# Retention and a softplus feed-forward on one core: five plain and three seven-product pairs of weight blocks in the first pass

## The chip, the cores and the metric

The kernel runs on one core of a Trainium2 chip. The metric is the device time of the whole program in microseconds (us), the median of three timed runs. Engines are called PE (TensorE's matmuls; PEld is its weight load), DVE (VectorE), ACT (ScalarE), POOL (GpSimd) and SP (SyncE, whose queue issues all the DMAs spoken of here). Each engine takes its instructions in the order in which the program has them.

## The reference

Causal retention (attention without softmax, with a decay per head) on 8 batches, 8 heads, 576 tokens, 64 columns per head, and on its result, seen as 4608 tokens by 512 features, a two-layer network with a softplus between:

```python
ret = (q @ k.transpose(0, 1, 3, 2) / np.sqrt(64)) * Dmat      # Dmat = gamma_h ** (i - j) for i >= j, else 0
x = (ret @ v).transpose(0, 2, 1, 3).reshape(4608, 512)
h = x @ w_in                                                  # w_in: 512 x 2048
g = np.maximum(h, 0.0) + np.log1p(np.exp(-np.abs(h)))         # softplus
out = g @ w_out                                               # w_out: 2048 x 512
```

All of it is in float32. For the matmuls every operand is split in a head that the PE takes whole and the rest (HI and LO), and a product is three: LO by HI, HI by LO, HI by HI.

## The kernel before

**Tiling.** The 4608 tokens are nine units of 512. Unit 0 runs while the weights are still being split. The units after it go two at a time: a super-step takes the units 2s+1 and 2s+2 and all 2048 hidden columns. The change touches the first super-step (units 1 and 2); units 3 to 8 run in `full_pair` and `full_phase` and are left as they are. The hidden columns are 16 blocks of 128, in eight pairs J.

**Plain slots and seven-product pairs.** For a plain pair, h is computed once per unit and block: `plain_slot(u, p, xa, xb, ...)` does two products (lines 847 to 851, six matmuls of 512 columns each) for block p of unit u, then the softplus on ACT and DVE, the split of g, and the output products (`output_some`, line 500, twelve matmuls) of the block before. That makes eight products for a pair and both units. `strassen_pair` computes the same four results (two blocks, two units) by Strassen and Winograd's scheme with seven products, from sums of x and sums of the weights. Its products are, in order, B11 and T2, T3, NT4 into the PSUM bank `acc`, B21 into `two`, T1 and B22 into `third`; ACT and DVE put them together in the four parts c[0] to c[3] and take the softplus of each. The results for unit 2 are written out to DRAM (`kept`) and fetched again in the second pass (`kept_parts`), which then has only their output products to do.

**The two passes.** The first pass is unit 1: plain slots p = 0 to 11 (the pairs 0 to 5, PLAIN = 6) and then the seven-product pairs 6 and 7. The second is unit 2: twelve plain slots and the kept parts of the two pairs. The retention for coming tokens is done in groups (`chunk_products`, lines 209 to 299), one in every second slot and one in each pair: its small matmuls write the scores into `two` and the sums into `third`; DVE empties them (`scores_out` L243, `halves_out` L429, `states_out` L271 to L281). A pair's group asks at its end for the next group's keys and values (`queue_steps`): keys at once, the other three loads one by one with the next products.

**Sums.** The seven-product scheme wants sums of x, made from `xs` by `combined_x` (L447 to L450, one column of 128 tokens at a time, on POOL) and split by `combined_parts` (ACT L454, DVE L455). It wants sums of the weights too: `w_in`'s for a pair in this super-step before the pair runs, all of `w_in`'s and `w_out`'s for units 3 to 8. A set of them is two additions of 128 by 512 (L633 or L648), four of 128 by 256 (L658 to L661), a head on ACT (L665, two), a rest on DVE (L669, two) and two stores of 512 KB (L677).

**What sets the order.** Engine queues follow the program text. Which of these steps stands in which slot is written out by hand in tables: `schedule((slot, step, ...), ...)` for the two passes, `extras` for the seven-product pairs. Weight blocks come through a ring of seven tiles (`block_load`, L619): each product, when it is issued, asks for the block seven products ahead. Tiles called quad are nine; DMAs take turns on eight semaphores, and one waits for the one before it on its own.

Of the kernel before, what the change touches and what calls it, by code (L numbers as in the profile page):

```python
# [54 lines left out]
PLAIN = 6  # L55
# [28 lines left out]
def retention_softplus_ffn(ctx: ExitStack, tc, first, whole, others, consts, w, out):  # L84
# [831 lines left out]
    def prepare_rest(j):  # L916
        combine_rest(raws[j])
# [25 lines left out]

    def start_combined(i, engine=nc.gpsimd):
        tmps[i] = quad().rearrange("p n (a b c) -> p (n a) b c", a=2, b=2)
        combined_x(tmps[i], column(i), engine)
# [10 lines left out]
    def half_b22(i):  # L957
# [5 lines left out]
        (1, prepare, PLAIN + 1), (1, prepare_whole, PLAIN), (2, prepare_sums, PLAIN), (3, prepare_split, PLAIN),  # L963
        (3, half_b22, 0), (4, prepare_store, PLAIN), (4, prepare_whole, PLAIN + 1), (4, prepare_sums, PLAIN + 1),
        (5, finish_combined, 0, nc.vector), (5, half_b22, 1), (6, prepare_split, PLAIN + 1),
        (6, prepare_ring, 4, 0, 3, 2), (7, prepare_store, PLAIN + 1), (7, prepare_ring, 4, 3, 4, 3),
        (7, finish_combined, 1, nc.vector), (7, half_b22, 2), (8, prepare_sums, 4), (9, prepare_ring, 5),
        (9, finish_combined, 2, nc.vector), (10, prepare_split, 4), (10, prepare_sums, 5), (10, half_b22, 3),
        (11, prepare_store, 4), (11, finish_combined, 3, nc.vector), (11, prepare_head, 5),
        (0, whole_out, 0), (1, combine_out, 0), (2, split_out, 0), (3, store_out, 0),  # L970
        *[(5 + 2 * j, raw_store, j) for j in range(4)])
    starts = schedule(*[(3 + 2 * i, start_combined, i) for i in range(CPU)])
    for p in range(2 * PLAIN):
        group = groups.pop() if p % 2 == 0 and p < 10 else None
        plain_slot(1, p, B11, B21, rest, group, (), *(x.get(p, ()) for x in (jobs, starts)))
# [6 lines left out]
    def strassen_pair(s, J, group, rest, last=False, extra=None):  # L982
# [12 lines left out]
        if extra is not None:  # L995
            whole_out(extra)
        for j in stores:
            prepare_rest(j)
        if last:
            half_x(B12, STAGE[0, 1], slice(0, T), nc.gpsimd)  # L1000
        ab = None if J == PLAIN else logs(c[0])
        output_some(-(-len(outputs) // 4))
        while stores:
            prepare_store(stores.pop(0))
        product(z, T1, True)
        nc.scalar.copy(c[1], z)  # L1006
        ab = ab or logs(c[0])
        softplus(c[0], ab)
        if extra is not None:
            combine_out(extra)  # L1010
        product(acc, T2)
        nc.scalar.copy(c[2], acc)
        if extra is not None:
            combine_head(raws["out", extra])
# [10 lines left out]
        if extra is not None:  # L1025
            combine_rest(raws["out", extra])
# [4 lines left out]
        nc.scalar.copy(c[3], acc)  # L1031
        ab4 = logs(c[3])
# [7 lines left out]
        if group:  # L1040
            chunk_products(*group, None)
            coming_steps = next_steps(group[0]) if s == 0 and J == NJ - 1 else []
            if extra is not None:
                combine_store(outs_dram[extra], raws.pop(("out", extra)))
            group_out(*group, between=(finish,))
            for k in coming_steps:
                scale_values(k)
# [14 lines left out]
    stores = [5]  # L1062
# [7 lines left out]
    extras = {(0, NJ - 2): 1, (0, NJ - 1): 2}  # L1070
    for s in range(FULL):
# [3 lines left out]
        for J in range(first, NJ):  # L1075
            rest, kept = strassen_pair(s, J, groups.pop() if groups else None, rest, s == 0 and J == NJ - 1,
                                       extras.get((s, J)))
# [10 lines left out]
        if first:  # L1088
            blocks = schedule((0, prepare_ring, 0))
            plan = schedule(  # L1090
                *[(2 * j - 1, prepare_ring, j) for j in range(1, 4)], *[(2 * j, prepare_sums, j) for j in range(4)],
                *[(2 * j + 1, prepare_split, j) for j in range(4)], *[(2 * j + 2, prepare_store, j) for j in range(4)],
                *[(8 + 2 * i, finish_combined, i, nc.vector) for i in range(2)],
                (9, half_x, B21, STAGE[1, 0], whole, nc.vector), *[(2 * j - 7, raw_store, j) for j in range(4, NJ)],
                (4, whole_in, 3, 0), (6, combine_out, 3), (7, split_out, 3), (8, store_out, 3),
# [318 lines left out]
```

## Time and profile before

| | |
|---|---|
| three timed runs | 834.57 us median (832.39 to 835.04) |
| the profiled execution's own time | 834.83 us, of which 833.0 us from the first to the last instruction |
| PE busy | 816.8 us (98%), 7322 instructions |
| DVE, ACT, POOL busy | 644.3 (77%), 546.8 (66%), 164.3 us (20%) |
| granted TensorE clock, mean | 0.998 |
| DMA | 209.93 MB, 252 GB/s |

Busy PE time counts overlapping matmuls whole, so short waits hide in it: how fast matmuls follow one another is read from the starts of a timeline's rows. A row with "x12" is twelve instructions merged, with the start of the first. What stands in brackets is idle time before it and what ended it. In the order rows below, a name is the tile, `xt` the split x, `xs` the x before the split, `quad` the tiles of sums and of c, `wout` the split `w_out`, `ab` and `g` the softplus before and after its split.

### The profile page before, as it was taken

What the parts mean: (1) busy time and instruction counts of PE and PEld (TensorE: products, weight loads), DVE (VectorE), ACT (ScalarE), POOL (GpSimd) and SP (SyncE); (2) the same over time, 40 slices, a digit from 0 to 9 for tenths busy, and PEclk for the clock granted to TensorE, in tenths of its full rate; (3) what the DMA queues carried; (4) which work ended last, traced back from release to release, by engine and by line L of the source; (5) the groups of instructions that cost most, each with busy time, mean ns of one, the idle gap of its engine ahead of it and who ended that gap; (6) DMA issues with size and microseconds to landing.
All of it is one profiled execution on the core that took longest, in us unless ns stands there. A gap on an engine that the chain in (4) does not pass through costs nothing.

```text
span 833.0 us, 19064 instructions
## 1 busy us (share of the span) xinstructions
PE 816.8 (98%) x7322; PEld 667.2 (80%) x7322; DVE 644.3 (77%) x1068; ACT 546.8 (66%) x957; POOL 164.3 (20%) x228
## 2 busy tenths in 40 slices
PE   8999999999999999999999999999999999999998
PEld 6788888887778888888887887888778888888886
DVE  5899976878787885878989985777789955555886
ACT  6788765456754544777777556767675658878653
POOL 3322221540221452111113000112110002212100
PEclk9999999999999999999999999999999999999999
DMA  9888879887799984697887777778657686666675
GB/s 357 311 284 304 314 247 359 293 300 247 244 317 343 334 281 150 221 307 253 284 267 260 215 228 235 252 235 261 195 159 213 205 254 190 195 194 193 194 214 172
DMA packets 149258, 209.93 MB, mean 252 GB/s; under 512 B 10800, under 2 KB 114736, under 8 KB 149168
## 3 DMA queue, kind: packets, MB, share of 16 engines
q1 hardware_dynamic: 149168, 208.72, 76.1%
q8 instruction: 58, 0.95, 0.4%
q14 instruction: 32, 0.26, 0.1%
HBM read 166.74 MB, written 41.94 MB: 251 GB/s over the span
## 4 chain that ended last, share of the span: by engine, by line
PE 73%; DVE 14%; ACT 8%; DMA 2%; issue 2%; SPq 0%; DVEq 0%; ACTq 0%
PE sum L1153 17%; PE acc L849 16%; PE y L500 12%; PE third L849 9%; PE two L849 4%; PE two L1153 3%; PE acc L1153 2%; PE third L1153 2%; PE h L466 2%; ACT ab L477 2%; PE third L225 2%; ACT parts L1143 2%; DVE g L1163 1%; DVE parts L1147 1%; ACT ab L473 1%
## 5 line engine op out<-in xcount | busy, mean ns | idle before, releaser
L849 PE MATMUL acc<-xt,ring 128*128 128x512 f32 x768 | 194.4, 391 | 1.0 <-DVE quad L1022 0.6
L1153 PE MATMUL sum<-parts,ring 128*128 128x512 f32 x720 | 174.9, 394 | 1.6 <-ACT ab L478 1.6
L849 PEld LDWEIGHTS acc<-xt,ring 128*128 128x128 f32 x768 | 143.9, 188 | 33.5 <-ACT g L1176 1.4
L1143 ACT CAST parts<-g 128x512 fp32r<-128x512 f32 x168 | 102.9, 621 | 88.5 <-DVE g L1163 28.4
L1153 PEld LDWEIGHTS sum<-parts,ring 128*128 128x128 f32 x720 | 134.6, 189 | 30.3 <-DVE xs L429 1.5
L1147 DVE TENSOR_TENSOR parts<-g,parts 128x512 fp32r<-128x512 f32 x168 | 117.7, 722 | 38.1 <-ACT parts L1143 36.2
L500 PE MATMUL y<-wout,g 128*128 128x512 f32 x576 | 140.1, 392 | 0.3 <-DVE g L493 0.3
L500 PEld LDWEIGHTS y<-wout,g 128*128 128x128 f32 x576 | 107.1, 188 | 23.3 <-PE h L466 0.7
L849 PE MATMUL third<-xt,ring 128*128 128x512 f32 x444 | 111.2, 390 | 0.0
L849 PEld LDWEIGHTS third<-xt,ring 128*128 128x128 f32 x444 | 83.2, 188 | 17.9 <-ACT quad L1006 0.4
L478 ACT ACTIVATE ab<-ab 128x512 f32<-128x512 f32 x120 | 75.9, 632 | 3.8
L477 ACT ACTIVATE ab<-ab 128x512 f32<-128x512 f32 x120 | 75.9, 633 | 3.5
L1163 DVE SCALAR_TENSOR_TENSOR g<-g,ab 128x512 f32<-128x512 f32 x96 | 67.4, 713 | 7.7 <-ACT ab L478 7.5
L202 POOL TENSOR_TENSOR qv<-qv,consts_sb 128x256 f32<-128x256 f32 x61 | 44.2, 726 | 116.9 <-DMA qv<-others 109.2
L489 ACT CAST g<-ab 128x512 fp32r<-128x512 f32 x44 | 27.3, 621 | 45.3 <-DVE ab L485 24.4
L466 PE MATMUL h<-xt,win 128*128 128x512 f32 x192 | 47.3, 395 | 1.3 <-DVE x L410 0.7
L493 DVE TENSOR_TENSOR g<-ab,g 128x512 fp32r<-128x512 f32 x44 | 32.7, 742 | 18.0 <-ACT g L489 17.2
L283 POOL TENSOR_TENSOR s<-s,consts_sb 128x256 f32<-128x256 f32 (+1 forms) x31 | 20.4, 657 | 127.2 <-DVE s L281 109.8
L473 ACT ACTIVATE ab<-g 128x512 f32<-128x512 f32 x72 | 45.0, 625 | 0.0
L849 PE MATMUL two<-xt,ring 128*128 128x512 f32 x168 | 42.8, 391 | 0.8 <-DVE xs L429 0.8
L1252 POOL TENSOR_TENSOR g<-g 128x512 f32<-128x512 f32 x10 | 14.1, 1409 | 149.1 <-DVE g L1163 149.1
L466 PEld LDWEIGHTS h<-xt,win 128*128 128x128 f32 x192 | 35.3, 188 | 9.4 <-DVE win L587 1.5
(191 smaller groups left out, 1340.5 us busy)
## 6 DMA issues: line engine op xcount, KB each, us to landing
ring<-split SPq DMA_DIRECT2D x126, 256.0 KB, 4.6
ring<-combined SPq DMA_DIRECT2D x104, 256.0 KB, 3.5
ring<-outcombined SPq DMA_DIRECT2D x96, 256.0 KB, 3.4
qv<-others SPq DMA_DIRECT2D x61, 320.0 KB, 4.9
ring<-outsplit SPq DMA_DIRECT2D x72, 256.0 KB, 3.6
wst<-w SPq DMA_DIRECT2D x32, 512.0 KB, 5.6
keys<-others SPq DMA_DIRECT2D x61, 256.0 KB, 5.1
split<-win SPq DMA_DIRECT2D x16, 512.0 KB, 6.0
```

What stands on the lines that cost most here:

```text
L202: nc.gpsimd.tensor_mul(v, v, f.unsqueeze(2).broadcast_to([P, 4, D]))
L466: nc.tensor.matmul(h, wins[p][:, a, kt * P:(kt + 1) * P], xt[:, b, T1 + kt // 2, kt % 2], start=(n == 0), stop=(n == 3 * NKT - 1))
L473: nc.scalar.activation(ab, h, AF.Abs)
L477: nc.scalar.activation(ab, ab, AF.Exp, scale=-1.0)
L478: nc.scalar.activation(ab, ab, AF.Ln, bias=1.0)
L493: nc.vector.tensor_sub(g[:, LO], ab, g[:, HI].bitcast(F32))
L500: nc.tensor.matmul(ys[u][tt], g[:, a, tt * P:(tt + 1) * P], wouts[p][:, b], start=(p == 0 and n == 0), stop=(p == NF - 1 and n == 2))
L849: nc.tensor.matmul(bank, w[:, ta, kt * P:(kt + 1) * P], xt[:, tb, x, kt], start=start and k == 0, stop=k == 5, skip_group_check=True)
L1143: nc.scalar.copy(t[:, HI], g_slot(J, n))
L1147: nc.vector.tensor_sub(t[:, LO], g_slot(J, n), t[:, HI].bitcast(F32))
L1153: nc.tensor.matmul(bank[m], w[:, a, m * P:(m + 1) * P], t[:, b], start=start and n == 0, stop=n == 2, skip_group_check=True)
L1163: nc.vector.scalar_tensor_tensor(c, c, 0.0, ab, op0=ALU.max, op1=ALU.add)
```

## The change

Five pairs are plain in the first super-step and three are seven-product pairs (5, 6 and 7). The sums of x are made on DVE, two columns of 128 tokens in one instruction (`start_wide`, `finish_wide`). The sums of `w_in` for pair 7 and those of `w_out` for pairs 1 to 4 are made inside the three seven-product pairs (`work`), up to two sets in each. Pair 4's `w_in` sums move to the second pass, and B12's rest in the last pair goes from POOL to DVE.

```diff
-PLAIN = 6
+PLAIN = 5
...
+    def start_wide(i, half):
+
+        b11, b12, b21, b22 = (later["xs"][:, STAGE[n], :, wide(i)] for n in ((0, 0), (0, 1), (1, 0), (1, 1)))
+        t = quad().rearrange("p n (b c) -> p n b c", b=2)
+        if half == 0:
+            nc.vector.tensor_sub(t[:, 0], b12, b11)
+            nc.vector.tensor_sub(t[:, 1], b22, b12)
+        else:
+            nc.vector.tensor_sub(t[:, 0], b22, tmps[i, 0][:, 0])
+            nc.vector.tensor_sub(t[:, 1], b21, t[:, 0])
+        tmps[i, half] = t
+
+    def finish_wide(i, half):
+        at = slice(T1 + 2 * half, T1 + 2 * half + 2)
+        hi, lo = (xt[:, n, at, :, wide(i)] for n in (HI, LO))
+        t = tmps[i, half]
+        nc.scalar.copy(hi, t)
+        nc.vector.tensor_sub(lo, t, hi.bitcast(F32))
+
+    def in_sums(j):
+        return [lambda f=f: f(j) for f in (prepare_whole, prepare_sums, prepare_head, prepare_rest, prepare_store)]
+
+    def out_sums(j):
+        return [lambda: whole_out(j), lambda: combine_out(j), lambda: combine_head(raws["out", j]),
+                lambda: combine_rest(raws["out", j]), lambda: store_out(j)]
...
-    starts = schedule(*[(3 + 2 * i, start_combined, i) for i in range(CPU)])
+        (9, finish_wide, 1, 0), (9, start_wide, 1, 1), (9, finish_wide, 1, 1), (9, half_b22, 3),
+        *[(3 + 2 * j, raw_store, j) for j in range(4)])
+    starts = {}
...
@@ strassen_pair @@
-        if extra is not None:
-            whole_out(extra)
-        for j in stores:
-            prepare_rest(j)
+        for f in work[0][:2] if work else ():
+            f()
         if last:
-            half_x(B12, STAGE[0, 1], slice(0, T), nc.gpsimd)
-        ab = None if J == PLAIN else logs(c[0])
+            half_x(B12, STAGE[0, 1], slice(0, T), nc.vector)
         output_some(-(-len(outputs) // 4))
-        while stores:
-            prepare_store(stores.pop(0))
         product(z, T1, True)
         nc.scalar.copy(c[1], z)
-        ab = ab or logs(c[0])
+        ab = logs(c[0])
         softplus(c[0], ab)
-        if extra is not None:
-            combine_out(extra)
         product(acc, T2)
         nc.scalar.copy(c[2], acc)
-        if extra is not None:
-            combine_head(raws["out", extra])
+        for f in work[0][2:3] if work else ():
+            f()
...
         softplus(c[2], ab2)
-        if extra is not None:
-            combine_rest(raws["out", extra])
+        for f in work[1][:2] if len(work) > 1 else ():
+            f()
...
         nc.scalar.copy(c[3], acc)
+        for f in work[1][2:3] if len(work) > 1 else ():
+            f()
         ab4 = logs(c[3])
...
-            if extra is not None:
-                combine_store(outs_dram[extra], raws.pop(("out", extra)))
             group_out(*group, between=(finish,))
+            for n in range(3, 5):
+                for fs in work:
+                    fs[n]()
...
-    extras = {(0, NJ - 2): 1, (0, NJ - 1): 2}
+    work = {(0, PLAIN): (in_sums(PLAIN + 2), out_sums(1)), (0, PLAIN + 1): (out_sums(2), out_sums(3)),
+            (0, PLAIN + 2): (out_sums(4),)}
...
@@ second pass @@
-                (4, whole_in, 3, 0), (6, combine_out, 3), (7, split_out, 3), (8, store_out, 3),
-                (8, whole_in, 4, 1), (9, combine_out, 4), (10, split_out, 4), (11, store_out, 4))
+                (9, prepare_head, 4), (9, stores.append, 4), (3, half_x, B21, STAGE[1, 0], whole, nc.vector),
```

Three places show how the instructions move. First ACT, from the last plain slot's softplus into the first seven-product pair; L990 and L1018 are the copy that empties `acc` after B11. Before:

```order
L478 ACTIVATE ab<-ab 128x512
L489 CAST g<-ab 128x512
L454 CAST xt<-quad 128x8x128
L665 CAST quad<-quad 128x512 x2
L990 COPY quad<-acc 128x512
L1006 COPY quad<-third 128x512
```

Now:

```order
L478 ACTIVATE ab<-ab 128x512
L489 CAST g<-ab 128x512
L963 CAST xt<-quad 128x4x256 x2
L434 CAST xt<-xs 128x2x128
L1018 COPY quad<-acc 128x512
L1029 COPY quad<-third 128x512
```

Two heads of sums of x and one of B22 stand ahead of the copy, where one head of x and two of weights stood; the second L963 needs a DVE result (L956) that is itself made in this slot. Second DVE, in the first seven-product pair, from the addition that frees `acc` for NT4 (L1022, L1043) to the next pair's first addition. Before:

```order
L1022 TENSOR_TENSOR quad<-acc,quad 128x512
L493 TENSOR_TENSOR g<-ab,g 128x512
L485 SCALAR_TENSOR_TENSOR ab<-quad,ab 128x512
L669 TENSOR_TENSOR quad<-quad 128x512 x2
L243 TENSOR_TENSOR a<-two,mask 128x512
L429 TENSOR_TENSOR xs<-two,consts_sb 128x4x128
L485 SCALAR_TENSOR_TENSOR ab<-quad,ab 128x512 x2
L279 COPY s<-third 128x256
L992 TENSOR_TENSOR quad<-two,quad 128x512
```

Now, from the softplus of c[2] (L485, left out here) on:

```order
L648 TENSOR_TENSOR quad<-wout_181 128x512
L648 TENSOR_TENSOR quad<-wout_182 128x512
L658 TENSOR_TENSOR quad<-quad 128x256
L659 TENSOR_TENSOR quad<-quad 128x256
L660 TENSOR_TENSOR quad<-quad 128x256
L661 TENSOR_TENSOR quad<-quad 128x256
L243 TENSOR_TENSOR a<-two,mask 128x512
L429 TENSOR_TENSOR xs<-two,consts_sb 128x4x128
L485 SCALAR_TENSOR_TENSOR ab<-quad,ab 128x512 x2
L279 COPY s<-third 128x256
L669 TENSOR_TENSOR quad<-quad 128x512 x4
L1020 TENSOR_TENSOR quad<-two,quad 128x512
```

Six additions of a second set of sums come ahead of L243 and L429, which empty `two`, and four rests (L669) stand where two stood, now behind the group's part. Third SP, in the same pair, with each DMA's waits (DMAHW0 to 7 are the eight semaphores in turn). Before:

```order
L1027 DMA kept_177<-ab 128x512 [waits DMAHW6_49,DVE_49]
L619 DMA ring<-split_122 128x2x256 [waits DMAHW7_49,PE_49]
L677 DMA outcombined_0_157<-quad 128x1024 [waits DMAHW0_49,DVE_49,Activation_49]
L677 DMA outcombined_1_158<-quad 128x1024 [waits DMAHW1_49,DVE_49,Activation_49]
L161 DMA keys<-others 128x512 [waits DMAHW2_49,PE_49]
L619 DMA ring<-split_107 128x2x256 [waits DMAHW3_49,PE_49]
L167 DMA qv<-others 128x640 [waits DMAHW4_49,Pool_49]
L619 DMA ring<-split_107 128x2x256 [waits DMAHW5_49,PE_49]
L167 DMA qv<-others 128x640 [waits DMAHW6_49,Pool_49]
L619 DMA ring<-split_108 128x2x256 [waits DMAHW7_49,PE_49]
L161 DMA keys<-others 128x512 [waits DMAHW0_49]
```

Now:

```order
L677 DMA combined_0_137<-quad 128x1024 [waits DMAHW2_49,DVE_49,Activation_49]
L677 DMA combined_1_138<-quad 128x1024 [waits DMAHW3_49,DVE_49,Activation_49]
L677 DMA outcombined_0_157<-quad 128x1024 [waits DMAHW4_49,DVE_49,Activation_49]
L677 DMA outcombined_1_158<-quad 128x1024 [waits DMAHW5_49,DVE_49,Activation_49]
L161 DMA keys<-others 128x512 [waits DMAHW6_49,PE_49]
L619 DMA ring<-split_121 128x2x256 [waits DMAHW7_49,PE_49]
L167 DMA qv<-others 128x640 [waits DMAHW0_49,Pool_49]
L619 DMA ring<-split_121 128x2x256 [waits DMAHW1_49,PE_49]
L167 DMA qv<-others 128x640 [waits DMAHW2_49,Pool_49]
L619 DMA ring<-combined_0_137 128x2x256 [waits DMAHW3_49,PE_49]
L161 DMA keys<-others 128x512 [waits DMAHW4_49]
```

Four stores of sums stand ahead of the next group's keys and values, where two stood, and the second values and second keys now wait on the semaphores of the first and third of these stores.

## Rows read from the trace of the kernel before

**Rows 1.** The page: engine's busy time and share; granted TensorE clock in 40 slices

```profile
PE 816.8 (98%) x7322; PEld 667.2 (80%) x7322; DVE 644.3 (77%) x1068; ACT 546.8 (66%) x957; POOL 164.3 (20%) x228
...
PEclk9999999999999999999999999999999999999999
```

**Rows 2.** PE's timeline, end of first pass: start, length, line, tiles, count

```profile
182.84 2.88 PE L500 MATMUL y<-wout,g 128*128 128x512 f32 x12
185.56 2.88 PE L849 MATMUL acc<-xt,ring 128*128 128x512 f32 x12
...
196.44 1.52 PE L849 MATMUL acc<-xt,ring 128*128 128x512 f32 x6
...
201.20 1.52 PE L849 MATMUL acc<-xt,ring 128*128 128x512 f32 x6
...
207.41 1.66 PE L849 MATMUL acc<-xt,ring 128*128 128x512 f32 x6 [0.61 <-DVE quad L1022]
...
211.02 0.96 PE L500 MATMUL y<-wout,g 128*128 128x512 f32 x3
212.08 1.66 PE L849 MATMUL acc<-xt,ring 128*128 128x512 f32 x6
...
230.89 3.00 PE L849 MATMUL two<-xt,ring 128*128 128x512 f32 x12 [0.82 <-DVE xs L429]
```

**Rows 3.** ACT's timeline, slots 9 to 11 and into pair 6

```profile
185.72 0.62 ACT L489 CAST g<-ab 128x512 fp32r<-128x512 f32 x1 [0.76 <-DVE ab L485]
186.25 1.05 ACT L454 CAST xt<-quad 128x1024 fp32r<-128x1024 f32 x1
...
193.04 0.40 ACT L434 CAST xt<-xs 128x256 fp32r<-128x256 f32 x1
...
199.12 0.58 ACT L990 COPY quad<-acc 128x512 f32<-128x512 f32 x1
```

**Rows 4.** DVE's timeline, slots 9 to 11

```profile
189.63 1.21 DVE L455 TENSOR_TENSOR xt<-quad,xt 128x1024 fp32r<-128x1024 f32 x1
190.77 0.68 DVE L485 SCALAR_TENSOR_TENSOR ab<-acc,ab 128x512 f32<-128x512 f32 x1
```

**Rows 5.** DVE's timeline in the pairs 6 and 7

```profile
200.34 1.28 DVE L648 TENSOR_TENSOR quad<-wout 128x512 f32<-128x512 f32 x2
...
204.49 0.42 DVE L658 TENSOR_TENSOR quad<-quad 128x256 f32<-128x256 f32 x1
...
206.08 0.68 DVE L1016 TENSOR_TENSOR quad<-third,quad 128x512 f32<-128x512 f32 x1
...
209.73 0.69 DVE L493 TENSOR_TENSOR g<-ab,g 128x512 fp32r<-128x512 f32 x1 [2.37 <-ACT g L489]
...
217.26 3.49 DVE L648 TENSOR_TENSOR quad<-wout 128x512 f32<-128x512 f32 x2
```

**Rows 6.** POOL's timeline in pair 7

```profile
217.05 2.55 POOL L437 TENSOR_TENSOR xt<-xs,xt 128x1024 fp32r<-128x1024 f32 x1 [1.13 <-ACT xt L434]
221.21 0.62 POOL L202 TENSOR_TENSOR qv<-qv,consts_sb 128x256 f32<-128x256 f32 x1 [1.60 <-DMA qv<-others]
```

**Rows 7.** ACT's timeline in pair 6: one softplus chain

```profile
207.24 0.62 ACT L473 ACTIVATE ab<-quad 128x512 f32<-128x512 f32 x1
207.90 0.63 ACT L477 ACTIVATE ab<-ab 128x512 f32<-128x512 f32 x1
208.56 0.63 ACT L478 ACTIVATE ab<-ab 128x512 f32<-128x512 f32 x1
```

**Rows 8.** SP's timeline in pair 7: when DMAs are issued

```profile
218.75 0.59 SPq L161 DMA_DIRECT2D keys<-others  x1
219.43 0.52 SPq L619 DMA_DIRECT2D ring<-split  x1
```

**Rows 9.** DMA issues: KB each, median us from issue to landing

```profile
keys<-others SPq DMA_DIRECT2D x61, 256.0 KB, 5.1
...
outcombined<-quad SPq DMA_DIRECT2D x10, 512.0 KB, 5.0
```

## Prediction on record

> **What bounds the kernel now.** I read the page first: PE is busy 98% of the span, DVE 77%, ACT 66%, and the granted clock stands in its top tenth in every slice [rows 1] (the higher of its two levels, 2.4 GHz), so no time is lost to the clock and none is to be won. Next PE's timeline, for how fast its matmuls follow one another: the twelve output matmuls from 182.84 are followed by the next row at 185.56 [rows 2], so a 512-column matmul costs 2.72 / 12 = 0.227 us as long as nothing is waited for. Last I put the two seven-product pairs on that scale. They run from 196.44 to the first product of the second pass at 230.89, 34.45 us [rows 2]. In them are 2 x 42 product matmuls and 12 + 24 output matmuls, 120 x 0.227 = 27.2 us, and two groups of small matmuls: from 207.41 + 1.36 + 0.11 = 208.88 to 211.02 one takes 2.1 us, two 4.3. So about 3.0 us of the pairs are waits, among them one for L1022 and one for L429, 0.61 and 0.82 in brackets [rows 2]; each wait also costs some 0.11 us more after it (the 1.66 instead of 1.52 of the row that follows one). PE sets the time, and what feeds it in the pairs is DVE's and ACT's queues.
>
> **What the change removes.** A plain pair is 8 x 6 matmuls for both units, a seven-product pair 7 x 6. One pair changes over: 6 x 0.227 = 1.36 us less on PE. The output matmuls and the groups (thirteen in both) stay. That is sure, and 0.16% of the time.
>
> **What it moves to DVE.** The sums of x leave POOL (16 instructions of 128 x 256 in each pass) and come to DVE as 8 of 128 x 512 in each pass. Two L648 of that size take 1.28 together [rows 5], so 0.60 each from start to start, 0.68 to the end: 4.8 us a pass. In the plain slots, where a softplus is needed only a slot later, I cost that at nothing; cover is the 5.4 us of PE work of a slot, and the last slot, where it runs out, is term (a). B12's rest goes from POOL to DVE. POOL's took 2.55 us, from 217.05 [rows 6], and DVE's two L648 from 217.26 took 3.49 instead of 1.28 [rows 5]; everything behind them in that pair came late, down to L429 before 230.89. The Trainium skill ("SBUF — State Buffer", Who interferes with whom) says that a DVE instruction with two SBUF inputs and a GpSimd instruction that reads SBUF block each other whole. By that rule DVE waits until POOL ends at 219.60 and is done 1.28 later, at 220.88; the trace has 220.75, so it agrees. By it the 0.82 wait for L429 goes; without it that wait could stay, and the sum below would be 0.9 higher.
>
> **The new waits, walked through the queues.** The old waits, 3.0 us, all lie where the program is rewritten, so I take them all off and count the new ones. Times are on the clock of before; the first seven-product pair (5) now starts at 185.56, where slot 10 started.
>
> (a) T2 of pair 5 goes into `acc`, which ACT must empty by L1018. ACT's cast of g in slot 9 is at 185.72, the next one starts at 186.25 and takes 1.05 [rows 3]: that is now the first L963, to 187.30. DVE's L964 follows, 1.14 until the next one starts [rows 4], then L955 and, on its result, L956, 0.72 and 0.68: 189.9. Now ACT's second L963, to 190.95; the next cast starts 0.95 after its start and takes 0.40 [rows 3], 191.26; L1018 takes 0.58 [rows 3]: 191.84. PE is at T2 at 185.56 + 2.72 (B11, B21) + 0.68 (three output matmuls) + 1.36 (T1) = 190.32. It waits until 191.9: 1.6 + 0.1. Before, the same copy ended at 199.70 for a T2 at 201.20 [rows 2, 3].
>
> (b) T3 waits for L1033, which stands behind a softplus chain of three activations, 0.66 apart [rows 7], begun after L1020 at 193.1: `acc` is free at 195.65, PE was there at 195.4. NT4 waits for L1043, which needs T3's end, with 0.68 us of PE work between: 0.26. Together 0.8 with what follows each.
>
> (c) B21 of pair 6 goes into `two`, which L429 empties. ACT's g is ready at 199.6, so DVE has L493 and L485 to 200.8, then the second set of sums: two L648, 1.2, and four of 256 columns, 0.46, 0.46, 0.34, 0.34 apart (L658 at 204.49 to L1016 at 206.08, 1.6) [rows 5]. That makes 203.6, L243 and L429 end at 204.9. PE: NT4 from 198.1, group, output, B11, at 203.8 ready for B21. Wait 1.2 + 0.1, and 0.2 at T1, whose bank the states free.
>
> (d) The group in pair 6 wants keys and values which are asked for after pair 5's group. Before, the second keys were issued at 218.75 [rows 8] and landed 5.1 later by the median [rows 9], 223.9, for a group that began at 226.5 (230.89 less the wait of 0.9, six output matmuls and the group's 2.1): 2.6 us to spare. Now SP stops at the four stores, which want the four L669. These come after the softplus of c[3], whose chain stands on ACT behind two more L665 (it ends at 206.8): L485, L279, then L669 ends at 208.6, 209.2, 209.8 and 210.4. Loads follow at 0.6 apart (218.75 to 219.43 [rows 8]) from 211.1 on; but the order has the second values wait on the semaphore of the first store (208.7 + 5.0 [rows 9] = 213.7) and the second keys on that of the third, 214.9. They land at 220.0 to 220.4. PE is at the group at 217.8 and at its second step 0.35 later: 2.2 + 0.1.
>
> (e) In pair 7 the same again: pair 6's rests end 228.0 to 229.8, the second keys land at 239.7 while PE comes at 238.2 + 0.35: 1.2 + 0.1. Just before, NT4 waits for L1043 behind DVE's last set and L437 of 1.14: 0.75 + 0.1. The wait before the second pass is gone.
>
> The second pass: six kept parts give PE 6 x 2.72 = 16.3 us of output matmuls, and DVE six rests of 0.60, two sums of x (1.2), two rests of sums of x and two of B11 and B22 (1.14 each) and two L669 (1.2), 10.6 us; I cost it at nothing, 0.2 at most where `half_x` and the last rests meet.
>
> **The sum.** 1.7 + 0.8 + 1.5 + 2.3 + 2.2 = 8.5 of new waits, less 3.0 of old ones, less 1.36: +4.1 us. The profiled execution took 834.83 us (span 833.0 and 1.8 around it), 0.26 above the median; +4.1 on the median gives 838.7, and I take 838.5, since a late group gives DVE time to catch up. Bounds: (d) and (e) hang on two landings in a row, for each of which I allow 1 us either way, so together they lie between 0.5 and 6; (a) to (c) between 2.5 and 5; POOL's L202, two in a pair, can hold DVE up by their own 0.62 each [rows 6], 1.5 us in all where DVE is late. The sum of the low ends is -1.4, of the likelier high ends +7: 833.2 to 841.6.
>
> **Rivals.** *The queues hold, no change.* If keys land in time and DVE's second sets are hidden, (a) and (b) are left with part of (c): 3.0 of waits for 3.0 before, and the 1.36 stays: 833.2 to 836. For it: DVE idled 2.37 us before L493 in the old pair [rows 5]. Against it: in that idle time ACT, not DVE, is awaited, and its chain isn't shortened. It decides if the first L669 ends before 206. Chance 0.27.
> *Faster.* Free of POOL, DVE runs ahead, and only the 0.3 waits of NT4 remain: 834.6 - 1.4 - 3.0 + 1.1 = 831.3. Against it stands (a), which is a chain without slack. Chance 0.07.
> *Slower by more: the ring runs dry.* The stores hold up the weight blocks behind them on SP too. A block is asked for seven products ahead, some 17 us; SP's stop is 8 to 10. Past 12 it would decide, at 2 to 3 us a pair: 842 to 845. Chance 0.06.
> The forecast, waits of 6 to 10 us in the three pairs, has 0.60.
>
> **How the numbers follow.** A measurement tells 0.3%, 2.5 us, from no change. Slower by more than that (over 837.1): the forecast's 0.60, less a little for its low end, plus the last rival's 0.06, 0.64. Faster (below 832.1): 0.06. Within: 0.30. Range 833.6 to 842.0; the forecast's own is 836.5 to 841.
>
> **What would show it.** In the changed profile: PE idle before an `acc` matmul released by L1018 at about 190 us, 1.6 us long (a); before `two` in the second pair, released by L429 (c); inside the groups of pairs 6 and 7, released by the load of keys or values, 1 to 2.5 us (d, e); none before the second pass's first product. Wrong would be: groups that begin on time, L669 before L429's successors reach PE, or twelve product matmuls not 0.227 apart.

## The result and the profile after

The changed kernel took 842.72 us (median of four, 841.42 to 843.83), the kernel before, run beside it, 833.58 (832.39 to 835.04): the ratio is 1.0100, with a 95% interval of 1.0076 to 1.0124. It is slower, as forecast, but by 9.1 us where 4 were forecast, and 0.7 us above the upper end of the range. Its profiled execution took 842.97 us, of which 840.9 span.

The page of the changed kernel, with the same two lines as [rows 1]:

```profile
PE 818.1 (97%) x7316; PEld 667.2 (79%) x7316; DVE 647.3 (77%) x1086; ACT 549.2 (65%) x960; POOL 133.4 (16%) x196
...
PEclk9999999999899999999999999999999999999999
```

PE has its six matmuls fewer, and yet 1.3 us more of busy time. The one digit that isn't 9 says where to look: in the slice from 210 to 231 us the granted clock isn't whole. PE's timeline through the three seven-product pairs and into the kept parts (start, length, line, tiles, count; in brackets the idle time before the row and what ended it), to be set beside [rows 2]:

```profile
188.10 1.52 PE L849 MATMUL third<-xt,ring 128*128 128x512 f32 x6
190.94 1.67 PE L849 MATMUL acc<-xt,ring 128*128 128x512 f32 x6 [1.32 <-ACT quad L1018]
...
194.82 1.65 PE L849 MATMUL acc<-xt,ring 128*128 128x512 f32 x6 [0.16 <-ACT quad L1033]
...
204.49 1.65 PE L849 MATMUL two<-xt,ring 128*128 128x512 f32 x6 [1.26 <-DVE xs L429]
...
213.28 1.66 PE L849 MATMUL acc<-xt,ring 128*128 128x512 f32 x6 [0.16 <-ACT quad L1033]
...
219.23 0.27 PE L225 MATMUL third<-qv,keys 64*64 64x64 f32 x1 [1.46 <-POOL qv L202]
...
221.84 0.34 PE L225 MATMUL third<-qv,keys 64*64 64x64 f32 x1 [2.15 <-DMA keys<-others]
...
225.03 2.93 PE L500 MATMUL y<-wout,g 128*128 128x512 f32 x6
227.75 1.62 PE L849 MATMUL acc<-xt,ring 128*128 128x512 f32 x6
229.21 1.52 PE L849 MATMUL two<-xt,ring 128*128 128x512 f32 x6
...
243.10 0.24 PE L225 MATMUL third<-qv,keys 64*64 64x64 f32 x1 [1.09 <-DMA keys<-others]
...
246.38 2.99 PE L849 MATMUL two<-xt,ring 128*128 128x512 f32 x12
...
321.19 2.12 PE L500 MATMUL y<-wout,g 128*128 128x512 f32 x8 [0.69 <-DVE g L493]
```

Each bracket has a term of the prediction beside it: L1018 is (a), L1033 is (b), L429 is (c), L202 and the keys at 221.84 are (d), the keys at 243.10 (e). The wait of [rows 2] before the second pass's first product is gone (246.38 has no bracket). What no term has is the row at 225.03: six matmuls take from 225.03 to 227.75 here, 0.453 each with the restart in the first, against 0.227 in the rows around it. The windows of the same stretch (from:to, length, then busy us of PE, PEld, DVE, ACT and POOL, the granted clock, DMA share, GB/s):

```profile
214.00:217.60 3.60, 3.60 (x17) 2.59 (x15) 2.07 (x4) 3.17 (x6) 0.00 (x0) 1.00 0.97 300
217.60:221.00 3.40, 0.63 (x17) 0.33 (x16) 2.99 (x4) 2.58 (x5) 1.82 (x2) 1.00 0.91 270
221.00:225.00 4.00, 3.16 (x96) 3.10 (x96) 1.95 (x5) 2.04 (x5) 0.10 (x1) 0.51 1.07 386
225.00:228.00 3.00, 3.00 (x9) 2.39 (x8) 2.83 (x6) 1.06 (x3) 0.39 (x1) 0.52 0.04 12
228.00:232.00 4.00, 4.00 (x19) 3.27 (x19) 3.97 (x7) 2.15 (x3) 0.92 (x1) 1.00 0.43 175
```

In the group PE stood for 1.46 and then 2.15 us with a few small matmuls between; after that the granted clock is at the lower of its two levels, 1.2 GHz, for nearly seven microseconds.

To set the kernels side by side I use one stretch: from the first product of the first pass to the first product of `full_pair`, everything that the change rewrites. It is 215.86 us before and 225.26 after, 9.4 more. The rest of the two profiled executions, outside it, differs by 1.5 the other way, so, as far as one execution of each can tell, the 9.1 us of the medians lie in the stretch. By term; measured are the waits alone, by the starts of the rows, (d) by its two brackets, and the forecast has in it the 0.1 or so that the restart behind each wait costs:

| term | forecast | measured |
|---|---|---|
| (a) T2 of pair 5 | 1.7 | 1.5 |
| (b) T3 and NT4 | 0.8 | 0.6 in pair 5, 0.3 in pair 6 |
| (c) B21 of pair 6, and T1 | 1.5 | 1.4, and 0.04 at T1 |
| (d) pair 6's group: values and keys | 2.3 | 3.6 |
| the lower clock behind it | – | 2.8 |
| (e) pair 7: NT4, keys | 0.85, 1.3 | 0, 1.2 |
| kept parts | 0 to 0.2 | 0.85 |

The clock's 2.8: what is left of the group takes 3.19 us (221.84 to 225.03), where a whole group takes 2.1 and its first step 0.35, so 1.44 more; and the six output matmuls take 2.72 instead of 1.36.

The measured terms add up to 12.3 us; less the 3.0 of old waits and the 1.36 of the six matmuls that is 7.9 of the 9.4. The rest is the restarts, some 0.13 in each row behind a wait (194.82 to 196.31 is 1.49 instead of 1.36), and what the brackets of (d) leave out: by the starts of the rows it is 4.0.

The queues stood as the prediction read them. ACT, slot 9 into pair 5 (beside [rows 3]), and DVE in pair 5, from the second set's additions to `two` and to the rests (beside [rows 5]):

```profile
185.39 1.05 ACT L963 CAST xt<-quad 128x1024 fp32r<-128x1024 f32 x1
189.06 1.05 ACT L963 CAST xt<-quad 128x1024 fp32r<-128x1024 f32 x1 [2.62 <-DVE quad L956]
190.01 0.40 ACT L434 CAST xt<-xs 128x256 fp32r<-128x256 f32 x1
190.31 0.58 ACT L1018 COPY quad<-acc 128x512 f32<-128x512 f32 x1
```

```profile
200.16 1.29 DVE L648 TENSOR_TENSOR quad<-wout 128x512 f32<-128x512 f32 x2
201.48 0.50 DVE L658 TENSOR_TENSOR quad<-quad 128x256 f32<-128x256 f32 x1
...
202.82 0.42 DVE L661 TENSOR_TENSOR quad<-quad 128x256 f32<-128x256 f32 x1
203.16 0.69 DVE L243 TENSOR_TENSOR a<-two,mask 128x512 f32<-128x512 f32 x1
203.76 0.68 DVE L429 TENSOR_TENSOR xs<-two,consts_sb 128x512 f32<-128x512 f32 x1
...
207.25 2.91 DVE L669 TENSOR_TENSOR quad<-quad 128x512 fp32r<-128x512 f32 x4
```

ACT idles 2.62 us for L956 and then has a second head and B22's ahead of the copy that PE is waiting for. DVE's L429 ends at 204.44, and PE's first product into `two` starts at 204.49. The forecast for the two ends was 191.84 and 204.9 on the clock of before; everything here runs 0.87 earlier, since this execution began its first product at 121.44 and that of before at 122.31. So they came out within 0.5.

SP's queue, behind the four L669 (beside [rows 8]):

```profile
207.99 1.34 SPq L677 DMA_DIRECT2D combined<-quad  x2
209.61 1.15 SPq L677 DMA_DIRECT2D outcombined<-quad  x2
210.85 1.10 SPq L161 DMA_DIRECT2D keys<-others  x1
212.05 1.16 SPq L619 DMA_DIRECT2D ring<-split  x1
213.29 0.60 SPq L167 DMA_DIRECT2D qv<-others  x1
213.99 0.52 SPq L619 DMA_DIRECT2D ring<-split  x1
...
215.83 0.59 SPq L161 DMA_DIRECT2D keys<-others  x1
```

The first keys stand there at 210.85, 0.6 later than forecast (211.1 less 0.87). They and the block behind them take 1.10 and 1.16, twice as long as others of their kind (0.59 and 0.52). The change didn't bring that: in the kernel before the same two, behind two stores, are nearly as long:

```profile
213.83 0.98 SPq L161 DMA_DIRECT2D keys<-others  x1
214.91 1.13 SPq L619 DMA_DIRECT2D ring<-split  x1
```

From the first keys to the second it is 4.98 us here and 4.92 there (213.83 to the 218.75 of [rows 8]), where the forecast had 3.8 (211.1 to 214.9). What lengthens these two rows no run shows. So the second keys leave SP from 215.83 instead of 214.0, and land at 221.71, 5.9 later instead of 5.1 [rows 9]; PE's row at 221.84 follows.

### The profile page after: what moved, and what is told of

Read it like the earlier page. It is cut to its first block, busy times and chain, and to the rows that moved or that the text cites. A ratio compares the mean times of both kernels' runs of the same rounds, so it can differ in the third digit from the quotient of the medians.

```text
span 840.9 us, 19048 instructions
## 1 busy us (share of the span) xinstructions
PE 818.1 (97%) x7316; PEld 667.2 (79%) x7316; DVE 647.3 (77%) x1086; ACT 549.2 (65%) x960; POOL 133.4 (16%) x196
## 4 chain that ended last, share of the span: by engine, by line
PE 85%; DVE 6%; DMA 4%; ACT 2%; issue 1%; SPq 1%; DVEq 0%
PE sum L1178 19%; PE acc L849 19%; PE y L500 12%; PE third L849 11%; PE two L849 5%; PE h L466 3%; PE two L1178 3%; PE third L225 2%; PE acc L1178 2%; PE third L1178 2%; PE two L287 2%; PE two L209 2%; DMA split<-win 2%; DMA keys<-others 1%; PE two L299 1%
## 5 line engine op out<-in xcount | busy, mean ns | idle before, releaser
L849 PE MATMUL third<-xt,ring 128*128 128x512 f32 x432 | 108.4, 390 | 0.0
L849 PEld LDWEIGHTS third<-xt,ring 128*128 128x128 f32 x432 | 80.9, 188 | 17.3 <-DVE s L279 0.3
L202 POOL TENSOR_TENSOR qv<-qv,consts_sb 128x256 f32<-128x256 f32 x61 | 47.2, 776 | 127.8 <-DMA qv<-others 127.7
L493 DVE TENSOR_TENSOR g<-ab,g 128x512 fp32r<-128x512 f32 x42 | 29.5, 702 | 15.8 <-ACT g L489 15.1
L225 PEld LDWEIGHTS third<-qv,keys 64*64 64x64 f32 x776 | 27.9, 136 | 16.3 <-issue 12.8
```

Of the source, the lines that this page charges most:

```text
L202: nc.gpsimd.tensor_mul(v, v, f.unsqueeze(2).broadcast_to([P, 4, D]))
L225: return nc.tensor.matmul(L["T"][rows[h], t, part[s]], L["kp"][rows[t], s, rows[h]], L["v"][rows[t], s, rows[h]], start=True, stop=True, s ...
L849: nc.tensor.matmul(bank, w[:, ta, kt * P:(kt + 1) * P], xt[:, tb, x, kt], start=start and k == 0, stop=k == 5, skip_group_check=True)
```

## The experiments

My theory after the two traces was that the loads behind the four stores cost most (3.6 us of wait, and the clock with it), the rival that DVE has no room for a second set of sums in a pair, and that the late loads only stand in front of that. Times are medians with the ratio to the kernel before, run on the same chip; "stretch" is the one defined above (before 215.86, after 225.26).

**The next group's loads ahead of the stores.** In the pairs 5 and 6 the stores of the sums go out behind the keys and values.

```diff
-            for n in range(3, 5):
-                for fs in work:
-                    fs[n]()
+            for fs in work:
+                fs[3]()
...
-            if not coming_steps:
+            if coming_steps:
+                for fs in work:
+                    fs[4]()
+            else:
                 queue_steps(group[0])
+                rest0, rest1, keys1 = queued[:3]
+                first_store, *later_stores = [fs[4] for fs in work]
+                queued[:3] = [lambda: (rest0(), rest1()), lambda: (keys1(), first_store()), *later_stores]
```

> Only the place of the stores changes: in the seven-product pairs 5 and 6 the next group's keys and values are asked for ahead of the four stores of sums. If late loads are the cause (my theory), the waits inside the groups of pairs 6 and 7 go (3.6 and about 1 us in the changed kernel's profile), and so does the stretch of 6.8 us at the lower clock, some 2.3 us of longer matmuls: 7 us less; part comes back, up to 3 us, as waits for DVE in pair 7 (B21, T1, NT4), which the late group had hidden: 836 to 839 us. Rival, DVE's queue is the cause and the late loads only stand in its shadow: pair 7 waits as long in other places, 841 to 843. Rival, DMA itself is full there (busy share 1.0 before the group): loads asked for earlier land no earlier, 841 to 843, with the group still waiting for keys.

841.28 us, 1.0075 [1.0051, 1.0099]; stretch 223.46. PE's waits in the three pairs (waiting tile and line, releaser: us in total, times, longest):

```profile
PE two L849 <- DVE xs L429: 2.0, 2, 1.3
PE acc L849 <- ACT quad L1033: 1.9, 2, 1.0
PE acc L849 <- ACT quad L1018: 1.3, 1, 1.3
PE acc L849 <- DVE quad L1043: 1.0, 1, 1.0
PE third L849 <- DVE s L281: 0.8, 1, 0.8
```

Nothing waits for keys or values, and the clock stays at its upper level throughout the pairs. That takes 3.6, 2.8 and 1.2 us away, 7.6 in all, and the stretch gained 1.8: T3 of pair 6 now waits 1.16 (0.32 without this edit), and in pair 7 B21, T1, T3 and NT4 wait 0.85, 0.94, 1.11 and 1.13, where there was nothing. These five waits are 4.9 us more; a good part of the 0.9 that is left is the restarts behind them, some 0.14 each. While PE stood for the keys, DVE caught up. The rival has most of it.

**The second pair of x sums a slot earlier.** `start_wide(1, 1)`, L955 and L956, in slot 8 instead of 9:

```diff
-        (9, finish_wide, 1, 0), (9, start_wide, 1, 1), (9, finish_wide, 1, 1), (9, half_b22, 3),
+        (8, start_wide, 1, 1), (9, finish_wide, 1, 0), (9, finish_wide, 1, 1), (9, half_b22, 3),
```

> Only the last sums of x (second half of the second two columns) move from slot 9 to slot 8. If T2 of pair 5 waits because ACT's copy L1018 stands behind a cast that wants them, its wait of 1.5 us and 0.1 after it goes, and DVE's queue in the pairs starts 2 to 3 us earlier, so stores and loads too: 1.5 to 3 us less, 839.5 to 841. Rival, the loads of pair 6 set the time whatever stands before them: the group of pair 6 waits that much longer, 842 to 843.

840.49 us, 1.0077 [1.0051, 1.0103]; stretch 223.07, 2.2 less. The wait for L1018 is gone, the one for L429 goes from 1.43 to 1.02, those for values and keys stay (1.45 and 2.43), and so does the lower clock behind them. (a) was a chain of its own, as the prediction had it.

**Both edits.** 

> Both edits, loads ahead of stores and the last sums of x in slot 8. If the two causes are separate, both gains: 834 to 837. If they are one (what is late in pair 5 is what makes the loads late), no more than the better of the two.

838.53 us, 1.0049 [1.0032, 1.0066]; stretch 220.92, 4.3 less than after: the gains of the two add up (1.8 and 2.2). What remains hangs on DVE's queue: 1.15 and 1.11 for L1033, 1.13 for L1043, 0.98 and 0.85 for L429, 0.95 for L281.

**Both, and the second set behind the group's part.** The second set's additions, which stand ahead of L243 and L429, are moved behind them, in the pairs 5 and 6:

```diff
-        for f in work[1][:2] if len(work) > 1 else ():
-            f()
...
-        for f in work[1][2:3] if len(work) > 1 else ():
-            f()
...
             group_out(*group, between=(finish,))
+            for f in work[1][:3] if len(work) > 1 else ():
+                f()
```

> Both edits, and the second set of sums of a pair (w_out's) is made after the group's scores and products are taken out of PSUM, not before. If B21 of pair 6 waits 1.4 us for L429 because of these six additions, it goes, and in pair 7 the like: 1 to 2.5 us less than with the two edits alone, 832 to 836, at or under the kernel before. Rival, DVE has no room anywhere in the pairs: the additions come back as a later L1020 and NT4 waits longer, the same time as with the two edits.

840.19 us, 1.0052 [1.0028, 1.0075]; stretch 221.39, no gain over the two edits alone. The waits of the pairs are gone but for 0.27 at NT4 of pair 5, and two others have come, at T2 of the pairs 6 and 7, of 2.3 and 4.2 us for L1018. The second of them in PE's timeline, and the windows around it:

```profile
230.40 2.01 PE L849 MATMUL acc<-xt,ring 128*128 128x512 f32 x6 [4.04 <-ACT quad L1018]
232.21 2.76 PE L849 MATMUL third<-xt,ring 128*128 128x512 f32 x6
```

```profile
226.00:231.00 5.00, 0.96 (x5) 0.52 (x4) 4.90 (x10) 2.79 (x5) 1.71 (x2) 1.00 0.62 225
231.00:234.40 3.40, 3.40 (x11) 2.59 (x10) 3.30 (x8) 3.05 (x6) 0.00 (x0) 0.57 1.03 346
```

DVE is busy 4.90 of 5.00 us while PE waits. In both places that were tried for the second set, PE pays for it; and where the wait is in one piece the clock takes its share again.

**One set in each pair, with both edits.** Only one set of weights' sums is made in each of the three pairs; the other two are made in the second pass (in the slots 3 to 6, and in the kept parts), and the last x sums start in slot 9 there.

```diff
-    work = {(0, PLAIN): (in_sums(PLAIN + 2), out_sums(1)), (0, PLAIN + 1): (out_sums(2), out_sums(3)),
-            (0, PLAIN + 2): (out_sums(4),)}
+    work = {(0, PLAIN): (in_sums(PLAIN + 2),), (0, PLAIN + 1): (out_sums(1),), (0, PLAIN + 2): (out_sums(2),)}
...
-                (9, start_wide, 1, 0), *[(2 * j - 7, raw_store, j) for j in range(4, NJ)])
+                (9, start_wide, 1, 0), (9, start_wide, 1, 1), *[(2 * j - 7, raw_store, j) for j in range(4, NJ)],
+                (3, whole_in, 3, 0), (4, combine_out, 3), (5, split_out, 3), (6, store_out, 3))
...
-            job((0, 0), start_wide, 1, 1)
...
+            job((1, 0), whole_in, 4, 1)
...
+            job((2, 0), combine_out, 4)
+            job((2, 0), split_out, 4)
+            job((2, 1), store_out, 4)
```

> Three seven-product pairs with one set of sums in each (w_in's for pair 7, w_out's for pairs 1 and 2), w_out's for pair 3 in the second pass's slots 3 to 6 and for pair 4 in its kept parts, besides the two edits before (loads ahead of stores, last sums of x early). If DVE's second set is what the pairs wait for (the rival of the first experiment, which its traces favour), the waits in the pairs fall from 5 to 6 us to 2 or 3, about what they were in the kernel before with two pairs, and the wait in the kept parts shrinks: 833 to 835.5, level with the kernel before or 1.4 under it. Rival, a seven-product pair costs its waits whatever stands in it (a chain of T3, L1043, NT4): 836 to 838.

831.21 us, 0.9962 [0.9948, 0.9975]; stretch 214.19, 11.1 less than after and 1.7 less than before. In the pairs one wait is left, 0.27 for L1043; two are new in the second pass, 1.24 for L281 in slot 7 and 0.52 for L493 in the kept parts.

**One set in each pair, alone.** The same without the two edits.

> The changed kernel with one set of sums in each pair (and the rest of w_out's in the second pass, as in e4_one_set), without the two other edits: stores still ahead of the next group's loads, last sums of x still in slot 9. If the second set on DVE is the cause of most of the loss, T2's wait of 1.5 us stays, B21's 1.4 goes, the rests and so the stores are done 2 to 3 us earlier and there are two of them instead of four, so keys and values land in time or within 1 us: 833 to 835.5. If the stores' place is a cause of its own, the groups still wait 1 us or more each, perhaps with the lower clock after them: 836 to 839.

834.66 us, 1.0028 [1.0012, 1.0044]; stretch 216.88, 8.4 less than after. The waits of all its pairs:

```profile
PE acc L849 <- ACT quad L1018: 1.3, 1, 1.3
PE acc L849 <- ACT quad L1033: 0.2, 1, 0.2
PE third L225 <- DMA keys<-others: 0.2, 1, 0.2
```

So the second set holds 8.4 of the 9.4 us of the stretch, the two new waits in the second pass (1.23 and 0.52) paid; by the medians, each against the kernel before beside it, 6.9 of 9.1 (834.66 against 832.47 here). With it go the wait for L429, nearly all of those for keys and values, and the lower clock. L1018's stays, since it has nothing to do with the weights. The edit takes the whole set out of the pair, its two heads on ACT and its two stores too; that DVE is the engine that is short is read from the traces (above, DVE is busy 4.90 of 5.00 us), not shown by an edit of its own.

**One set, the earlier x sums, and the stores ahead of the loads again.** 

> As e4_one_set but with the stores ahead of the next group's loads again: one set a pair and the last sums of x early. If two stores that come in time cost nothing, as e8_one_alone's trace (no wait in the groups) says, the same as e4: ratio 0.995 to 0.997. If the loads' place still matters, groups wait 0.5 to 1 us: 0.997 to 0.999.

831.27 us, 0.9988 [0.9970, 1.0005]; stretch 214.61, against 214.19 with the loads first. With one set, two stores stand ahead of the loads, and these come in time: the order of loads and stores, 1.8 us in the changed kernel, is worth 0.4 at most here.

**The x sums back on POOL.** The sums of x (8 of 128 x 512 in each pass) on POOL, beside the earlier slot; it is to be compared with the earlier slot alone.

```diff
-            nc.vector.tensor_sub(t[:, 0], b12, b11)
-            nc.vector.tensor_sub(t[:, 1], b22, b12)
+            nc.gpsimd.tensor_sub(t[:, 0], b12, b11)
+            nc.gpsimd.tensor_sub(t[:, 1], b22, b12)
...
-            nc.vector.tensor_sub(t[:, 0], b22, tmps[i, 0][:, 0])
-            nc.vector.tensor_sub(t[:, 1], b21, t[:, 0])
+            nc.gpsimd.tensor_sub(t[:, 0], b22, tmps[i, 0][:, 0])
+            nc.gpsimd.tensor_sub(t[:, 1], b21, t[:, 0])
```

> The changed kernel with the sums of x of both passes back on POOL, as wide as they are now, and the last ones in slot 8 as in e2_wide_early. If the move to DVE is a gain, POOL's two halves of the last columns, some 1.5 to 2.5 us each instruction, end after T2 is due and T2 waits again, 1 to 4 us, over e2: 842 to 845. If the engine doesn't matter, as e2: 839 to 841.

849.11 us, 1.0175 [1.0151, 1.0199]; stretch 232.00, 8.9 more than with the same sums on DVE. T2 of pair 5 waits again, 2.8 us by the starts of the rows; the keys cost 6.2 us in two waits, the longest 3.13, and two stretches at the clock's lower level follow, one behind that wait and one in the kept parts behind a wait of 2.8 for L493. The move to DVE is a part of the change that pays.

**The kernel before, with its x sums on DVE.** Both the sums of x and B12's rest, as in the change; the pairs as before.

```diff
-    def start_combined(i, engine=nc.gpsimd):
+    def start_combined(i, engine=nc.vector):
...
-            half_x(B12, STAGE[0, 1], slice(0, T), nc.gpsimd)
+            half_x(B12, STAGE[0, 1], slice(0, T), nc.vector)
```

> The kernel before with one part of the change alone: sums of x (one column at a time, as before) and B12's rest on DVE instead of POOL; six plain pairs and two seven-product pairs as before. The wait of 1.0 us before the second pass, which follows L648 stretched beside POOL's L437, goes if the two contend for a port; otherwise the sums hide in the plain slots: 833 to 834.5 (before 834.6). If DVE has no room for them in the plain slots: 835 to 838.

833.48 us, 0.9992 [0.9973, 1.0011]; stretch 214.94, 0.9 less: the wait for L429 before the second pass, 0.99 by the starts of the rows, is gone and the others stay. DVE's timeline in pair 7 of it, where [rows 5] had 3.49 for the same two L648:

```profile
218.24 1.28 DVE L648 TENSOR_TENSOR quad<-wout 128x512 f32<-128x512 f32 x2
219.45 1.21 DVE L437 TENSOR_TENSOR xt<-xs,xt 128x1024 fp32r<-128x1024 f32 x1
```

With POOL idle the two take 1.28, and the rest that took POOL 2.55 [rows 6] takes DVE 1.21. The rule of the Trainium skill ("SBUF — State Buffer", Who interferes with whom), by which a DVE instruction with two SBUF inputs and a GpSimd instruction that reads SBUF block each other, would give the 1.28 with POOL idle, and the trace agrees.

**The second pass spread out further.** From the best version so far, two ways to get at its wait of 1.24 for L281. The first moves twelve steps of the second pass, most of them by one slot or one output step (the sums of `w_out` a slot earlier, B21's rest two later, and so on):

```diff
-                (9, prepare_head, 4), (9, stores.append, 4), (3, half_x, B21, STAGE[1, 0], whole, nc.vector),
-                (6, start_wide, 0, 0), (6, start_wide, 0, 1), (7, finish_wide, 0, 0), (8, finish_wide, 0, 1),
+                (9, prepare_head, 4), (9, stores.append, 4), (5, half_x, B21, STAGE[1, 0], whole, nc.vector),
+                (6, start_wide, 0, 0), (7, start_wide, 0, 1), (8, finish_wide, 0, 0), (8, finish_wide, 0, 1),
...
```

> As e4_one_set, with three steps of the second pass moved so that no slot there gives DVE more than it has: the second half of the first sums of x to slot 7, w_out's set for pair 3 a slot earlier, B21 to slot 5, B11 and B22 and the last rests a kept part later. e4's trace has two waits left in that pass, 1.24 us for L281 behind four sums of x in slot 6, and 0.52 us for L493 in the first kept part; both should go, 1.5 to 2 us: 829 to 830. Rival, another slot overflows in its place: 831, as e4.

834.61 us, 1.0034 [1.0019, 1.0049]; stretch 217.42, 3.2 worse than the version that it starts from. The wait for L281 is gone, and others come: 1.76 that ends at 263.62, 1.0 in the kept parts for L493 (0.52 without the edit), 0.9 for L1209, and 0.9 in two for L347. A miss.

The second moves only the split of one set and its store a slot earlier:

```diff
-                (3, whole_in, 3, 0), (4, combine_out, 3), (5, split_out, 3), (6, store_out, 3))
+                (3, whole_in, 3, 0), (4, combine_out, 3), (4, split_out, 3), (5, store_out, 3))
```

> As e4_one_set, with the split of w_out's set for pair 3 in slot 4 of the second pass instead of slot 5. In e4's trace DVE leaves slot 5 late (three sorts of rests and sums in a slot that has a group too), so the sums of slot 6 stand ahead of the states and PE waits 1.24 us for L281. That wait should fall to 0.3 or go: ratio to the kernel before 0.995. Rival, as in e7_spread another wait of 1 to 2 us turns up in the next slots: 0.996 to 0.999.

834.12 us, 1.0020 [1.0002, 1.0039]; stretch 217.76, 3.6 worse, a miss again, and one that can be read whole. PE's one wait of that stretch, ACT's timeline there, and a window behind the wait:

```profile
PE third L225 <- ACT mark L347: 3.4, 1, 3.4
```

```profile
272.98 1.14 ACT L665 CAST sums<-sums 128x512 fp32r<-128x512 f32 x2 [3.94 <-DVE sums L661]
274.02 0.59 ACT L473 ACTIVATE ab<-acc 128x512 f32<-128x512 f32 x1
274.51 0.15 ACT L347 COPY mark<-third 128x1 f32<-128x1 f32 x1
```

```profile
276.00:280.00 4.00, 4.00 (x14) 3.13 (x13) 2.71 (x6) 0.06 (x1) 0.61 (x1) 0.68 0.78 235
```

The heads L665 now stand in ACT's queue ahead of L347, a copy of one column that a group's matmuls wait for, and themselves wait for eight additions on DVE. 1.24 us are won at L281, 3.4 lost at L347, and 1.5 more to the clock, at its lower level behind the wait.

**The best version once more, on another chip.** 

> The kernel of e4_one_set once more, in another job: it had 0.996 of the kernel before [0.9948, 0.9975], and e10_no_loads, which differs only in that the stores of pairs 5 and 6 stand ahead of the next group's loads, 0.9988 [0.9970, 1.0005] in a job of its own. In the traces of the two the stretch from slot 0's first product to the first product of the full pairs differs by 0.4 us (214.19 and 214.61), 0.05%. Theory: the two are the same within 0.1%, and the difference of the ratios is that of jobs: the ratio here lies between 0.996 and 0.999, and the stretch is 214.2 again. Rival: the order of loads and stores is worth 0.2% that the traces of single runs don't show: the ratio is 0.996 or lower once more, while the stretch stays at 214.2.

831.55 us, 0.9992 [0.9977, 1.0006]; stretch 214.15. The kernel's own median is that of the first time (831.21), but the kernel before took 832.78 here and 834.55 there. The rival is out. That a version with one set beats the kernel before is shown for the stretch (214.2 twice, 214.6 for its sister, against 215.86), and for the whole time on one of two chips, by 0.4%; on the other the interval holds no change.

## Why the prediction was right in its direction, and short by half

**Right.** The saving of six matmuls, the waits (a), (b) and (c) with their releasers and sizes, the end of the wait before the second pass, and that loads behind four stores come too late. (b) came a second time, in pair 6, where the sum had it once. Each was read by walking one queue, and the runs took three of the waits away by edits: (a) by an earlier slot, (c) and (d) by leaving out the second set. POOL's part was right as well: DVE does the sums of x at a price that the plain slots hide, and POOL's would have cost 8.9 us more.

**The step that failed.** "[T]he granted clock stands in its top tenth in every slice [...], so no time is lost to the clock and none is to be won." That holds of the pairs of the kernel before, whose waits are short. I forecast a wait of 2.2 us in a group, and priced it as if the matmuls behind it would run at 0.227 us as ever. They ran at 0.43 to 0.45, and with the rest of the group that is 2.8 us, the largest missing term. The trace of before held a hint that the prediction passed over: there too the granted clock is at its lower level for 3.4 us, from 587.8 on, behind a gap of 2.0 us in a group, which one digit for a slice of 21 us doesn't show.

**The term mis-sized: (d), 3.6 instead of 2.3, or 4.0 by the starts of the rows.** I followed the second keys alone. The first values came late too: asked for at 213.29, landed at 218.02, and then through POOL's L202, which took 1.09 instead of 0.62 [rows 6] beside DVE:

```profile
218.09 1.09 POOL L202 TENSOR_TENSOR qv<-qv,consts_sb 128x256 f32<-128x256 f32 x1 [9.68 <-DMA qv<-others]
```

And the second keys came 2.4 later than forecast. Most of that could be read in the trace of before, from the same loads in the same place: the 4.92 us from the first keys to the second, where I had 3.8, and 6.0 us to landing (224.73), where I took the 5.1 that is the median of the whole run. The semaphore of the third store, by which I had timed the second keys, held nothing up: that store landed at 213.07, the keys were asked for at 215.83. The 2.6 us to spare that I gave this group were 1.7: it began at 226.39. Of the terms costed near nothing, the kept parts took 0.85; NT4 in pair 7, costed at 0.85, took nothing, because DVE had caught up while PE waited for the keys.

**What the sum hid.** I added waits of one engine as though they were independent, and set "a late group gives DVE time to catch up" against them as a small change. It is the main one: of the 7.6 us that went with the late loads, all but 1.8 came back, most of it in waits behind DVE's queue. The cause under (c), (d) and (e) is one, the second set of sums in a pair, six additions and two rests on DVE, 4.4 us by the starts of the rows of after (1.3, 1.7, and half of the 2.83 from the first L669 to the row behind the four); without it 8.4 of the 9.4 us are gone. My rival "the queues hold" asked for the first L669 to end before 206; it began at 207.25, and the four ended at 210.2.

## What to carry to other kernels

A wait that you forecast on the matmul engine has a second price: look what the granted clock did behind the longest waits that the trace already shows, and add the slower matmuls to the sum. The time from issue to landing is to be read from the same load at the same place, not from the median of the run. When several waits have one engine's queue behind them, cost the work that was added to that queue, not the waits one by one; removing the wait that is longest in the trace mostly uncovers the next. A ratio of a few tenths of a per cent wants a second chip: here the same two kernels gave 0.996 and 0.999.

## What the runs showed of the hardware that I had not expected

- Behind waits on PE of 1.46 and 2.15 us close together (after; 1.45 and 2.43 with the earlier slot), of 2.8 and 3.1 (x sums on POOL), 3.4 and 4.0 us the granted clock went to the lower of its two levels, in the changed kernel from 221.1 to 227.9, and 512-column matmuls took 0.427 us each instead of 0.227. Behind a single wait of 2.3 in the pairs, and shorter ones, it stayed; it stayed as well behind 3.02 us for keys that ended at 223.25 with the x sums on POOL, so the length of a wait alone doesn't tell. Behind the 1.9 to 2.2 us in a group near 588 it fell in some kernels (before, after) and not in others.
- Where a load stands in SP's queue changes its time to landing: asked for behind stores of sums, keys landed 5.2 and 6.0 us after their issue in the kernel before (two stores ahead of them) and 5.7 and 5.9 in the changed one (four); asked for ahead of the stores, the first keys behind pairs 5 and 6 landed after 3.7 and 4.0. The median of the whole run before is 5.1.
- A POOL instruction beside DVE lengthens both: L648 3.49 for 1.28, L202 1.09 for 0.62.
